# Second-layer low products in bf16, a dense plane for the weights' high part, and one ring of six raw-weight buffers

## The chip, the cores and the metric

The kernel runs on one core of a Trainium2 chip. The metric is the device time of one execution in microseconds (us); before the change it is 961.33 us, the median of three runs (959.22 to 962.11). The core's engines are named as the profile names them: PE (TensorE, matrix products), PEld (the weight loads of PE), DVE (VectorE), ACT (ScalarE), POOL (GpSimd) and SP (the engine that issues most DMAs).

## The reference

Attention with a hash mask, then a two-layer network with a squared ReLU, all in float32. Shapes: 4 batches, 8 heads, 768 rows, head size 64; the network has 3072 rows, width 512 and 2048 hidden columns.

```python
mask   = bucket(q) == bucket(k)                  # 6 hash bits of each row
scores = where(mask, 0.125 * q @ k.T, -1e9)
attn   = softmax(scores)
x      = (attn @ v) reshaped to 3072 x 512
h      = x @ w_in                                # first layer, 512 -> 2048
g      = s * relu(h)**2 + b
out    = g @ w_out                               # second layer, 2048 -> 512
```

## The kernel before, in words

Every value that enters a product is split into a high and a low part, so that a product of two float32 matrices becomes three products of narrower types: high by high, high by low, low by high. The weights come from memory as pairs of 32-bit words and are put together on the chip ("decoded").

The rows of one batch are cut into three chunks of 256. For each chunk the first layer (lines 788 to 790, f16, 256 moving columns) makes 256 hidden columns ("a pair" of 128) in one PSUM bank with 24 products. ACT then forms the square and writes the high part `gh` (lines 798 to 800, tile `ghb`), and POOL writes the low part `gl` (lines 801 and 802, tile `glb`). The second layer (line 815) adds the pair into two PSUM banks, one for each 128 rows: 12 products of 512 moving columns, where a slice of `gh` or `gl` is loaded as PE's weights and a row block of `w_out` moves through: 8 with `gh` (against the high and the low part of `w_out`), 4 with `gl` (against the high part). All 12 are in float32r ("fp32r"), which the profile's rows call f32. There are 96 pairs: 4 batches, 3 chunks, 8 pairs.

Attention (lines 485 to 743) runs beside it: scores (lines 615 and 616, fp32r, 384 columns), softmax on DVE, ACT and POOL, and the product with the values (lines 686 and 692, f16). Once the attention of all heads is done, only the two layers of the last chunks are left; this is the tail from about 798 us on.

All instructions are collected as steps with an estimated cost, a priority and the keys that they read and write. The class `Plan` simulates the engines with these costs, picks at each moment the ready step of the best priority, and the steps are issued in that order. A step with several ways (a copy on ACT, POOL or DVE) goes to the engine that would end it first. Costs therefore set the order: a second-layer product is entered as 0.2343 (line 817).

`decode(u, pr)` (line 358) loads and decodes one of 32 row blocks of weights, in four groups of eight: four of `w_in`, then four of `w_out`. The raw block of `w_in` lives in a ring of six buffers (`wr0` to `wr5`) until the whole group's scale is known and it is split into f16 (lines 427 to 432). The raw block of `w_out` lives in the buffer that its decoded form takes later (`w{u}`), so it needs no ring. Its decoded form is one tile of two float32r planes, high and low (lines 399 to 401). The load is issued by ACT's queue (line 377), and two loads at most are open at a time (`PACE`).

Of the kernel before, what the change touches and what calls it, by code (L numbers as in the profile page):

```python
# [11 lines left out]
F32R = mybir.dt.float32r  # L12
I32 = mybir.dt.int32
F16 = mybir.dt.float16
BF16 = mybir.dt.bfloat16
U32 = mybir.dt.uint32
AF = mybir.ActivationFunctionType
ALU = mybir.AluOpType
# [11 lines left out]
PE, DVE, ACT, POOL, SP = (mybir.EngineType.PE, mybir.EngineType.DVE, mybir.EngineType.Activation,  # L30
                          mybir.EngineType.Pool, mybir.EngineType.SP)
# [137 lines left out]
def lsh_attention_moe(ctx: ExitStack, tc, q, k, v, proj, w_in, w_out, s, b, out):  # L169
    nc = tc.nc  # L170
    B, H, S, D = q.shape
    DM, DF = w_in.shape
    P = 128
# [3 lines left out]
    CH = 256  # L177
    NCH = S // CH
    TPC = CH // P
    NC_ = DM // P  # L180
# [7 lines left out]
    wk = ctx.enter_context(tc.tile_pool(name="wk", bufs=1))  # L188
# [5 lines left out]
    plan = Plan()  # L194

    def f32(ap):
        return ap.bitcast(F32)

    def tile_(name, shape, dt=F32):
        return const.tile(shape, dt, name=name)  # L200

# [4 lines left out]
    def pe(cost, fn, r, w, pr):  # L206
        plan.add(PE, cost, fn, r, w, pr)
# [16 lines left out]
    def copy(n, out, src, r, w, pr, ways, slow=0.0):  # L224

        def fn(e):
            o, x = out(), src()
            (e.copy if e is nc.scalar else e.tensor_copy)(o, x)
        some(n, fn, r, w, pr, ways, slow)
# [52 lines left out]
    xsb = tile_("xsb", [P, 2, CH], F16)  # L282
    rb = tile_("rb", [P, 2 * CH])
    ghb = tile_("ghb", [P, 2, 2 * CH], F32R)
    glb = tile_("glb", [P, 2, 2 * CH], F32R)
    osb = tile_("osb", [P, 2, DM])
    pt = tb[:, 2].rearrange("p a h t q -> p (a h t q)")[:, 0:4 * DM].bitcast(F32).rearrange("p (t c) -> p t c", t=2)
    NST = 2
# [61 lines left out]
    dec, wt, held_raw = [], {}, []  # L350
# [7 lines left out]
    def decode(u, pr):  # L358
        src, key = dec[u]
        box = {}  # L360
        wi, kin = key[0] == "wi", u // (NC_ + 4) * NC_ + key[-1]
        tag = f"wr{kin % NWR}" if wi else f"w{u}"

        def new():
            box["t"] = wk.tile([P, 512, 2], I32, tag=tag, name=f"raw{u}")
# [1 line left out]
        def raw():  # L367
            return box["t"]

        def words(z):  # L370
            return box["t"].rearrange("p n t -> p (n t)")[:, z * 512:(z + 1) * 512]
        rk, wk_ = [("raw", tag)], [key + (0,), key + (1,)]
        g, gk = osb[:, u % 2, :], ("os", u % 2)
        gi = g.bitcast(I32)
        held = ["pjs"] if u == ND - 1 else []
        plan.add(None, 0.0, new, [], rk + held, pr - 5)
        plan.add(ACT, 0.1, lambda: nc.scalar.dma_start(raw(), src.rearrange("p (n t) -> p n t", t=2)), GATE(KK, AK) if u < PACE else [], rk + [("pace", u % PACE)], pr - 5, 524288 / RATE_DMA)
        plan.moves.add(len(plan.steps) - 1)
        if wi:
            n, j = key[1:]  # L380
# [13 lines left out]
        dve(512, lambda: nc.vector.scalar_tensor_tensor(sum_(), gi, 3, words(0), ALU.logical_shift_left, ALU.bitwise_or), [], rk + [gk], pr, 0.75)  # L394
        if not wi:
            def swap():
                wt[key] = wk.tile([P, 2, 512], F32R, tag=f"w{u}", name=f"w{u}")
            plan.add(None, 0.0, swap, [], rk + wk_, pr)
            copy(512, lambda: wt[key][:, 0], lambda: g, [gk], [key + (0,)], pr, (ACT, POOL))
            plan.any([(POOL, 1.4, lambda: nc.gpsimd.tensor_tensor(wt[key][:, 1], g, f32(wt[key][:, 0]), ALU.subtract)),  # L400
                      (DVE, 0.7, lambda: nc.vector.tensor_tensor(wt[key][:, 1], g, f32(wt[key][:, 0]), ALU.subtract))], [gk, key + (0,)], [key + (1,)], pr)
            return
        held_raw.append((words, rk, key))
        if j < NC_ - 1:
# [355 lines left out]
    def moe(bb, c, g0=0, g1=NF // 4):  # L760
        boxes = []
        fa, fz = 4 * g0, 4 * g1
        pr = 1e5 + 100.0 * nu[0]
# [12 lines left out]
        for f0 in range(fa, fz, 2):  # L776
            while nd[0] < f0 // 4 * 8 + 6 + f0 % 4:
                yield
            u = nu[0] % 2
            nu[0] += 1  # L780
            fill = 1e5 + 100.0 * nu[0]
            for j in range(2):
                hp, fs = bank[:, 5, j * CH:(j + 1) * CH], slice((f0 % 4 + j) * P, (f0 % 4 + j + 1) * P)
                for cc in range(NC_):
                    def mm(cc=cc, hp=hp, fs=fs, n=f0 // 4):
                        xc = boxes[cc][0]["t"][:, boxes[cc][1]]
                        w = wt[("wi", n, cc)]
                        nc.tensor.matmul(hp, w[:, 0, fs], xc[:, 0, :], start=(cc == 0), stop=False)  # L788
                        nc.tensor.matmul(hp, w[:, 1, fs], xc[:, 0, :], start=False, stop=False)  # L789
                        nc.tensor.matmul(hp, w[:, 0, fs], xc[:, 1, :], start=False, stop=(cc == NC_ - 1))  # L790
                    pe(0.327, mm, [boxes[cc][2], ("wi", f0 // 4, cc, 0), ("wi", f0 // 4, cc, 1)], [("b", 5)], fill)
            r, rk = rb, "r"
            gh, gl, hk, lk = ghb[:, u], glb[:, u], ("gh", u), ("gl", u)
            g4 = f0 // 4
            ds, dk = dsc[:, bb, g4:g4 + 1], ("ds", bb, g4)
            if c == 0 and f0 % 4 == 0:
                dve(1, lambda g4=g4, ds=ds: nc.vector.tensor_tensor(ds, vsc[:, bb, 1:2], wsc[:, g4, 1:2], ALU.mult), [("sc", bb), ("wsc", g4)], [dk], MP, 0.1)
            some(2 * CH, lambda e, r=r, ds=ds: e.activation(r, bank[:, 5, :], AF.Relu, scale=ds) if e is nc.scalar else e.tensor_scalar(r, bank[:, 5, :], ds, 0.0, ALU.mult, ALU.max), [("b", 5), dk], [rk], MP, (ACT, DVE))  # L798
            act(2 * CH, lambda r=r: nc.scalar.activation(r, r, AF.Square), [], [rk], MP)
            act(2 * CH, lambda r=r, gh=gh: nc.scalar.activation(gh, r, AF.Identity, bias=b_sb, scale=s_sb), [rk, "sb"], [hk], MP, 0.15)  # L800
            pool(2 * CH, lambda r=r: nc.gpsimd.tensor_scalar(r, r, s_sb, b_sb, ALU.mult, ALU.add), [hk, "sb"], [rk], MP, 0.77)  # L801
            pool(2 * CH, lambda r=r, gh=gh, gl=gl: nc.gpsimd.tensor_tensor(gl, r, f32(gh), ALU.subtract), [rk, hk], [lk], MP)  # L802

            end = bb == B - 1 and c == NCH - 1 and f0 == NF - 2
            for part in ((0, 1), (2,)) if HALVES and not end else ((0, 1, 2),):
                for jt in range(2 * TPC):
                    j, t = (jt % 2, jt // 2) if end else (jt // TPC, jt % TPC)
                    f = f0 + j

                    def mm2(f=f, j=j, t=t, gh=gh, gl=gl, part=part):  # L810
                        ts = slice(j * CH + t * P, j * CH + (t + 1) * P)
                        o = bank[:, 6 + t, :]
                        w = wt[("wo", f)]
                        for z in part:
                            nc.tensor.matmul(o, (gh, gh, gl)[z][:, ts], w[:, z % 2], start=(f == fa and z == 0), stop=(f == fz - 1 and z == 2))  # L815
                    ks_ = [[hk, ("wo", f, 0)], [("wo", f, 1)], [lk]]
                    pe(0.2343 * len(part), mm2, [k for z in part for k in ks_[z]] + [("wo", f, 0)], [("b", 6 + t)], fill + 150)
        for t in range(TPC):
            o, os_ = bank[:, 6 + t, :], osb[:, t]
            if fz < NF:  # L820
# [36 lines left out]
    for i in range(NSL):  # L857
        pr = 10.0 * i
        bb, h, c, w = slots[i]
# [31 lines left out]


FIRST = 0.5
CONV = (ACT, POOL)
CONVCOST = 0.95
RATE = 1.0
# [4 lines left out]
NWR = 6  # L901
# [46 lines left out]
```

## Time and profile before

| | us |
|---|---|
| median of three runs | 961.33 |
| lowest and highest | 959.22, 962.11 |
| the profiled execution | 960.13 |
| its span | 958.3 |
| PE busy | 921.6 (96%) |
| DVE, ACT, POOL busy | 606.2, 656.7, 614.2 |

The span is the time from the first to the last instruction of the program; 1.8 us of the profiled execution lie around it. A busy PE is not a PE at its peak: a product's record lasts until its results have drained, so records of products that follow each other overlap. How fast PE really goes is read from the distance between the starts of two products.

### The profile page before, as it was taken

How to read it: one execution, taken by the hardware profiler on the slowest of the kernel's cores; microseconds unless marked ns; L12 is line 12 of the kernel's file. 1: busy time of each engine (PE TensorE's matmuls, PEld its weight loads, DVE VectorE, ACT ScalarE, POOL GpSimd, SP SyncE). 2: the span in 40 equal slices, each digit the busy share in tenths (PEclk: the TensorE clock that was granted, in tenths of full speed). 3: DMA queues.
4: the chain of work that ended last, by engine and by line, in shares of the span. 5: the costliest groups of instructions: out<-in, count | busy, mean ns of one | idle time of the engine just before them, and what ended most of it. 6: DMA issues, size and time to landing. Idle time of an engine off the chain costs nothing.

```text
span 958.3 us, 18093 instructions
## 1 busy us (share of the span) xinstructions
PE 921.6 (96%) x6512; PEld 733.2 (77%) x6512; DVE 606.2 (63%) x1001; ACT 656.7 (69%) x1234; POOL 614.2 (64%) x706
## 2 busy tenths in 40 slices
PE   7999887999999999999999999999999999999997
PEld 5876666677667777877878778788778887888886
DVE  7688997888777777776767676768777752000000
ACT  3788886778786777677778777767777775444342
POOL 2467775686896756766777676767667775334332
PEclk8999999899999999999999999999999999999999
DMA  5378657647779898997898798888887875100000
GB/s 123 87 232 220 177 160 191 179 133 209 174 153 204 176 206 181 204 213 149 157 204 172 163 204 163 177 174 167 186 173 149 171 134 105 55 19 27 12 23 23
DMA packets 303721, 144.44 MB, mean 151 GB/s; under 512 B 264256, under 2 KB 286784, under 8 KB 303632
## 3 DMA queue, kind: packets, MB, share of 16 engines
q1 hardware_dynamic: 298432, 126.25, 60.5%
q10 hardware_dynamic: 5200, 17.05, 5.7%
q8 instruction: 51, 0.84, 0.3%
q14 instruction: 38, 0.31, 0.1%
HBM read 51.38 MB, written 14.16 MB: 68 GB/s over the span
## 4 chain that ended last, share of the span: by engine, by line
PE 70%; DVE 9%; POOL 7%; ACT 5%; issue 5%; DMA 2%; POOLq 0%; SPq 0%; ACTq 0%; DVEq 0%
PE bank L815 22%; PE bank L788 7%; PE bank L790 7%; PE bank L789 7%; PE bank L615 6%; PE bank L616 5%; PE bank L686 4%; PE bank L680 3%; PE bank L672 2%; PE bank L692 2%; POOL eb L640 2%; DVE st L620 2%; PE bank L485 2%; POOL glb L802 2%; ACT eb L621 1%
## 5 line engine op out<-in xcount | busy, mean ns | idle before, releaser
L640 POOL TENSOR_SCALAR eb<-eb,st 128x768 f32<-128x768 f32 x176 | 200.4, 1145 | 68.4 <-DVE st L631 51.8
L815 PE MATMUL bank<-w,ghb 128*128 128x512 f32 x768 | 213.6, 406 | 0.0
L788 PE MATMUL bank<-xc,wi 128*128 128x256 f16 x768 | 211.6, 276 | 0.3 <-ACT rb L798 0.3
L620 DVE TENSOR_REDUCE st<-bank 128x1 f32<-128x768 f32 x192 | 180.3, 952 | 49.6 <-PE bank L616 42.3
L790 PE MATMUL bank<-xc,wi 128*128 128x256 f16 x768 | 209.7, 273 | 0.0
L789 PE MATMUL bank<-xc,wi 128*128 128x256 f16 x768 | 209.7, 273 | 0.0
L621 ACT ACTIVATE eb<-bank,st 128x768 f32<-128x768 f32 x176 | 157.5, 896 | 65.2 <-DVE st L620 29.3
L801 POOL TENSOR_SCALAR rb<-rb,misc 128x512 f32<-128x512 f32 x96 | 84.8, 884 | 154.0 <-ACT ghb L800 146.4
L648 DVE SCALAR_TENSOR_TENSOR pb<-eb,pb 128x768 f16<-128x768 f32 x132 | 144.3, 1097 | 61.5 <-ACT pb L647 60.9
L798 ACT ACTIVATE rb<-bank,dsc 128x512 f32<-128x512 f32 x95 | 65.2, 687 | 149.1 <-PE bank L790 135.4
L615 PE MATMUL bank<-ks,aq 128*128 128x384 f32 x384 | 146.7, 382 | 10.8 <-ACT eb L621 5.2
L815 PEld LDWEIGHTS bank<-w,ghb 128*128 128x128 f32 x768 | 136.1, 189 | 21.2 <-issue 0.4
L802 POOL TENSOR_TENSOR glb<-rb,ghb 128x512 fp32r<-128x512 f32 x96 | 137.1, 1428 | 5.8
L616 PE MATMUL bank<-ks,bq 76*128 76x384 f32 x384 | 132.1, 344 | 0.8 <-DMA bq<-nat 0.8
L647 ACT ACTIVATE pb<-eb 128x768 f16<-128x768 f32 x132 | 110.1, 836 | 14.3 <-DMA tb<-pb 13.3
L815 PE MATMUL bank<-w,glb 128*128 128x512 f32 x384 | 113.0, 402 | 3.1 <-POOL glb L802 3.1
L788 PEld LDWEIGHTS <-wi 128*128 128x128 f16 x768 | 75.0, 98 | 44.5 <-issue 37.3
L615 PEld LDWEIGHTS bank<-ks,aq 128*128 128x128 f32 x384 | 74.5, 194 | 30.0 <-ACT eb L621 9.2
L838 DVE COPY osb<-bank 128x256 f32<-128x256 f32 x4 | 1.5, 420 | 133.7 <-PE bank L815 133.0
L815 PEld LDWEIGHTS bank<-w,glb 128*128 128x128 f32 x384 | 70.8, 189 | 19.5 <-POOL glb L802 4.9
L625 POOL TENSOR_SCALAR st<-st 128x2 f32<-128x2 f32 x96 | 41.8, 436 | 63.2 <-DVE st L620 58.4
L790 PEld LDWEIGHTS <-wi 128*128 128x128 f16 x768 | 75.2, 98 | 8.6
(137 smaller groups left out, 1510.2 us busy)
## 6 DMA issues: line engine op xcount, KB each, us to landing
ks<-aq SPq DMA_DIRECT2D x60, 192.0 KB
raw<-in_moe_w_in_dram ACTq DMA_DIRECT2D x16, 512.0 KB
raw<-in_moe_w_out_dram ACTq DMA_DIRECT2D x16, 512.0 KB
xc<-xd SPq DMA_DIRECT2D x60, 128.0 KB
nat<-in_q_dram SPq DMA_DIRECT2D x32, 192.0 KB
nat<-in_k_dram SPq DMA_DIRECT2D x32, 192.0 KB
vm<-in_v_dram SPq DMA_DIRECT2D x32, 192.0 KB
xd<-xsb SPq DMA_DIRECT2D x48, 128.0 KB
```

Source lines behind the costliest of these rows:

```text
L615: nc.tensor.matmul(o, aq[:, ts], ks[0][:, cols], start=True, stop=False)
L616: nc.tensor.matmul(o, bq[0:HR, ts], ks[1][0:HR, cols], start=False, stop=True)
L620: dve(S, lambda a=a, sc=sc: nc.vector.tensor_reduce(nm[:, a:a + 1], sc, AX.XY, ALU.max, negate=True), bk, [nk[a]], pr, 0.88)
L621: act(S, lambda a=a, sc=sc, e=e: nc.scalar.activation(e.rearrange("p (g n) -> p g n", g=2), sc, AF.Exp, bias=nm[:, a:a + 1], accum_out=z[: ...
L640: eng.tensor_scalar(e, e, rz[:, a:a + 1], u[:, a:a + 1], ALU.mult, ALU.add)
L647: act(S, lambda e=e, hi=hi: nc.scalar.mul(hi, e, TOP), [ek], [hk], pr)
L648: dve(S, lambda e=e, hi=hi, lo=lo: nc.vector.scalar_tensor_tensor(lo, e, TOP, hi, ALU.mult, ALU.subtract), [ek, hk], [("lo", n)], pr, 1.0)
L788: nc.tensor.matmul(hp, w[:, 0, fs], xc[:, 0, :], start=(cc == 0), stop=False)
L789: nc.tensor.matmul(hp, w[:, 1, fs], xc[:, 0, :], start=False, stop=False)
L790: nc.tensor.matmul(hp, w[:, 0, fs], xc[:, 1, :], start=False, stop=(cc == NC_ - 1))
L802: pool(2 * CH, lambda r=r, gh=gh, gl=gl: nc.gpsimd.tensor_tensor(gl, r, f32(gh), ALU.subtract), [rk, hk], [lk], MP)
L815: nc.tensor.matmul(o, (gh, gh, gl)[z][:, ts], w[:, z % 2], start=(f == fa and z == 0), stop=(f == fz - 1 and z == 2))
```

## The change

Line numbers behind the change are 4 to 6 higher than before (the second layer's line 815 becomes 821, the first layer's 788 to 790 become 794 to 796, the raw load's 377 becomes 381).

- `gl` is written as bf16. `w_out` is decoded into three tiles: the high part `w` in float32r, the low part `wl` in bf16, and `wp`, the high part once more in bf16, made by one copy more.
- High by high stays in float32r. High by low takes the upper 16 bits of each word of `gh`, read with a step of two (`top`), as bf16 weights against `wl`. Low by high is `gl` against `wp`, bf16 against bf16.
- The planner's cost of the two bf16 products is 0.2165 instead of 0.2343.
- All 32 raw blocks share the ring of six (`u % 6`). So a load waits until the block six places before it is done with.

```diff
+    def top(ap):
+        return ap.bitcast(BF16).rearrange("p (n t) -> p n t", t=2)[:, :, 1]
...
-    glb = tile_("glb", [P, 2, 2 * CH], F32R)
+    glb = tile_("glb", [P, 2, 2 * CH], BF16)
...
-        wi, kin = key[0] == "wi", u // (NC_ + 4) * NC_ + key[-1]
-        tag = f"wr{kin % NWR}" if wi else f"w{u}"
+        wi = key[0] == "wi"
+        tag = f"wr{u % NWR}"
...
-                wt[key] = wk.tile([P, 2, 512], F32R, tag=f"w{u}", name=f"w{u}")
-            plan.add(None, 0.0, swap, [], rk + wk_, pr)
-            copy(512, lambda: wt[key][:, 0], lambda: g, [gk], [key + (0,)], pr, (ACT, POOL))
+                wt[key] = [wk.tile([P, 512], dt, tag=f"{x}{u}", name=f"{x}{u}") for x, dt in (("w", F32R), ("wl", BF16), ("wp", BF16))[:2 + PLANE]]
+            plan.add(None, 0.0, swap, [], held + wk_, pr)
+            copy(512, lambda: wt[key][0], lambda: g, [gk], [key + (0,)], pr, (ACT, POOL))
...
+            if PLANE:
+                copy(512, lambda: wt[key][2], lambda: g, [gk], [key + (2,)], pr, (ACT, POOL, DVE))
...
-                            nc.tensor.matmul(o, (gh, gh, gl)[z][:, ts], w[:, z % 2], start=(f == fa and z == 0), stop=(f == fz - 1 and z == 2))
-                    ks_ = [[hk, ("wo", f, 0)], [("wo", f, 1)], [lk]]
-                    pe(0.2343 * len(part), mm2, [k for z in part for k in ks_[z]] + [("wo", f, 0)], [("b", 6 + t)], fill + 150)
+                            nc.tensor.matmul(o, (gh, top(gh), gl)[z][:, ts], (w[0], w[1], w[2] if PLANE else top(w[0]))[z], start=(f == fa and z == 0), stop=(f == fz - 1 and z == 2))
+                    ks_ = [[hk, ("wo", f, 0)], [("wo", f, 1)], [lk, ("wo", f, 2 if PLANE else 0)]]
+                    pe(sum((0.2343, 0.2165, 0.2165)[z] for z in part), mm2, [k for z in part for k in ks_[z]] + [("wo", f, 0)], [("b", 6 + t)], fill + 150)
```

On PE, in the tail, the second layer of one pair stands like this before (`w_2354` and `w_2398` are two row blocks of `w_out`, both planes in one tile):

```order
L790 MATMUL bank<-xc_2_1_0_9363,wi_3_235 128x256
L815 MATMUL bank<-w_2354,ghb 128x512 x4
L815 MATMUL bank<-w_2398,ghb 128x512 x4
L815 MATMUL bank<-w_2354,glb 128x512 x2
L815 MATMUL bank<-w_2398,glb 128x512 x2
L788 LDWEIGHTS wi_0_232
```

and its middle like this now, at the same place (`w_253` is a block's high plane, `wl_254` its low one, `wp_252` the dense bf16 plane of the pair's other block):

```order
L821 MATMUL bank<-w_253,ghb 128x512
L821 LDWEIGHTS ghb
L821 MATMUL bank<-wl_254,ghb 128x512
L821 MATMUL bank<-w_253,ghb 128x512
L821 LDWEIGHTS ghb
L821 MATMUL bank<-wl_254,ghb 128x512
L821 LDWEIGHTS glb
L821 MATMUL bank<-wp_252,glb 128x512
```

A float32r product carries its weight load in itself; a 16-bit product has one of its own ahead of it. Twelve float32r products in a row have become four that alternate with bf16 ones, and then four bf16 ones, of which the first is shown.

On ACT, in the decoding of the first group, the third load of a `w_out` block (`raw_209`) stood right behind the decoding of the first (`raw_207`):

```order
L386 ACTIVATE osb<-raw_207 128x512
L377 DMA raw_208<-in_moe_w_out_dram 128x1024
L386 ACTIVATE raw_207<-raw_207 128x512
L228 COPY xpb<-bank 64x128
L586 ACTIVATE vm,vmx<-vm 128x384
L228 COPY xpb<-bank 64x128
L621 ACTIVATE pb,st<-bank,st 128x768
L621 ACTIVATE eb,st<-bank,st 128x768
L228 COPY tb<-bank 128x512 x3
L377 DMA raw_209<-in_moe_w_out_dram 128x1024
```

Now the third and fourth (`raw_1293`, `raw_1308`) stand some thirty rows further on, behind the split of the group's `w_in` blocks (`wi_1_204` and `wi_2_205`):

```order
L433 ACTIVATE wi_1_204<-raw_200,wsc 128x512
L433 ACTIVATE wi_2_205<-raw_201,wsc 128x512
L627 ACTIVATE eb,st<-bank,st 128x768 x2
L232 COPY tb<-bank 128x512 x3
L381 DMA raw_1293<-in_moe_w_out_dram 128x1024
L381 DMA raw_1308<-in_moe_w_out_dram 128x1024
```

The two loads moved behind the split, because they take the buffers of the first two `w_in` blocks.

## Rows read from the trace of the kernel before

**Rows 1.** The page: span, and busy time of each engine

```profile
span 958.3 us, 18093 instructions
PE 921.6 (96%) x6512; PEld 733.2 (77%) x6512; DVE 606.2 (63%) x1001; ACT 656.7 (69%) x1234; POOL 614.2 (64%) x706
```

**Rows 2.** Stretches: length, PE, PEld, DVE, ACT, POOL busy; granted clock, DMA share, GB/s

```profile
0.00:300.00 300.00, 270.42 (x2042) 209.67 (x2043) 245.88 (x474) 225.00 (x479) 206.32 (x253) 0.97 0.66 172
300.00:798.00 498.00, 496.60 (x3443) 398.05 (x3440) 354.22 (x517) 364.58 (x656) 346.85 (x393) 1.00 0.85 175
798.00:958.00 160.00, 154.58 (x1031) 125.45 (x1030) 6.10 (x11) 67.10 (x99) 61.05 (x61) 1.00 0.13 35
```

**Rows 3.** The same for line 815 alone, first stretch: length, PE busy, PEld busy

```profile
0.00:300.00 300.00, 35.83 (x120) 20.98 (x120) 0.97 0.66 172
```

**Rows 4.** The page's groups of line 815: busy us, mean ns, idle before

```profile
L815 PE MATMUL bank<-w,ghb 128*128 128x512 f32 x768 | 213.6, 406 | 0.0
...
L815 PE MATMUL bank<-w,glb 128*128 128x512 f32 x384 | 113.0, 402 | 3.1 <-POOL glb L802 3.1
```

**Rows 5.** Timeline of PE, one pair of the tail: start, length, instruction

```profile
881.78 0.27 PE L790 MATMUL bank<-xc,wi 128*128 128x256 f16 x1
881.81 2.10 PE L815 MATMUL bank<-w,ghb 128*128 128x512 f32 x8
883.74 1.10 PE L815 MATMUL bank<-w,glb 128*128 128x512 f32 x4
884.69 0.29 PE L788 MATMUL bank<-xc,wi 128*128 128x256 f16 x1
884.81 0.27 PE L789 MATMUL bank<-xc,wi 128*128 128x256 f16 x1
```

**Rows 6.** Timeline of PE, fp32r products alone between f16 ones

```profile
691.79 0.60 PE L686 MATMUL bank<-tb,vb 128*128 128x256 f16 x4
692.15 0.48 PE L815 MATMUL bank<-w,glb 128*128 128x512 f32 x1
...
692.59 0.27 PE L789 MATMUL bank<-xc,wi 128*128 128x256 f16 x1
```

**Rows 7.** Timeline of PE, two fp32r products between f16 ones

```profile
907.28 0.27 PE L790 MATMUL bank<-xc,wi 128*128 128x256 f16 x1
907.31 0.71 PE L815 MATMUL bank<-w,ghb 128*128 128x512 f32 x2
...
907.98 0.27 PE L789 MATMUL bank<-xc,wi 128*128 128x256 f16 x1
```

**Rows 8.** Timeline of PEld, the weight load behind a run of fp32r products

```profile
884.21 0.19 PEld L815 LDWEIGHTS bank<-w,glb 128*128 128x128 f32 x1
884.68 0.10 PEld L788 LDWEIGHTS <-wi 128*128 128x128 f16 x1 [0.28 <-issue]
```

**Rows 9.** Timeline of PE, f16 products whose weight tile changes its width

```profile
261.82 0.60 PE L686 MATMUL bank<-tb,vb 128*128 128x256 f16 x4
262.35 0.52 PE L692 MATMUL bank<-tb,vb 128*64 128x256 f16 x6
```

**Rows 10.** Timeline of ACT and POOL, the making of gh and gl in the tail

```profile
883.53 0.82 ACT L800 ACTIVATE ghb<-rb,misc 128x512 fp32r<-128x512 f32 x1
885.30 1.27 POOL L802 TENSOR_TENSOR glb<-rb,ghb 128x512 fp32r<-128x512 f32 x1
```

**Rows 11.** Groups by form, copies and subtraction in the decoding of w_out

```profile
L401 DVE TENSOR_TENSOR w<-osb,w 128x512 fp32r<-128x512 f32 x7 | 6.6, 949 | 0.5 <-ACT w L228 0.3 <-POOL w L228 0.2
...
L228 POOL CAST w<-osb 128x512 fp32r<-128x512 f32 x8 | 6.0, 748 | 2.9 <-DVE osb L394 1.5 <-ACT aq L487 1.4
...
L228 ACT CAST w<-osb 128x512 fp32r<-128x512 f32 x8 | 5.0, 620 | 1.3 <-POOL w L400 1.1
```

**Rows 12.** Timeline of ACT: third w_out load, and the first group's split

```profile
76.63 0.33 ACTq L377 DMA_DIRECT2D raw<-in_moe_w_out_dram  x1
...
112.32 1.95 ACT L427 ACTIVATE wi<-raw,wsc 128x512 f16<-128x512 f32 x3 [0.41 <-DVE wsc L447]
```

More of the change, by code (lines that the diff above doesn't have):

```diff
@@ L371, in words @@
             return box["t"].rearrange("p n t -> p (n t)")[:, z * 512:(z + 1) * 512]
-        rk, wk_ = [("raw", tag)], [key + (0,), key + (1,)]
+        rk, wk_ = [("raw", tag)], [key + (z,) for z in range(3)]
         g, gk = osb[:, u % 2, :], ("os", u % 2)
@@ L375, in decode @@
         held = ["pjs"] if u == ND - 1 else []
-        plan.add(None, 0.0, new, [], rk + held, pr - 5)
+        plan.add(None, 0.0, new, [], rk, pr - 5)
         plan.add(ACT, 0.1, lambda: nc.scalar.dma_start(raw(), src.rearrange("p (n t) -> p n t", t=2)), GATE(KK, AK) if u < PACE else [], rk + [("pace", u % PACE)], pr - 5, 524288 / RATE_DMA)
@@ L396, in swap @@
             def swap():
-                wt[key] = wk.tile([P, 2, 512], F32R, tag=f"w{u}", name=f"w{u}")
-            plan.add(None, 0.0, swap, [], rk + wk_, pr)
-            copy(512, lambda: wt[key][:, 0], lambda: g, [gk], [key + (0,)], pr, (ACT, POOL))
-            plan.any([(POOL, 1.4, lambda: nc.gpsimd.tensor_tensor(wt[key][:, 1], g, f32(wt[key][:, 0]), ALU.subtract)),
-                      (DVE, 0.7, lambda: nc.vector.tensor_tensor(wt[key][:, 1], g, f32(wt[key][:, 0]), ALU.subtract))], [gk, key + (0,)], [key + (1,)], pr)
+                wt[key] = [wk.tile([P, 512], dt, tag=f"{x}{u}", name=f"{x}{u}") for x, dt in (("w", F32R), ("wl", BF16), ("wp", BF16))[:2 + PLANE]]
+            plan.add(None, 0.0, swap, [], held + wk_, pr)
+            copy(512, lambda: wt[key][0], lambda: g, [gk], [key + (0,)], pr, (ACT, POOL))
+            plan.any([(POOL, 1.4, lambda: nc.gpsimd.tensor_tensor(wt[key][1], g, f32(wt[key][0]), ALU.subtract)),
+                      (DVE, 0.7, lambda: nc.vector.tensor_tensor(wt[key][1], g, f32(wt[key][0]), ALU.subtract))], [gk, key + (0,)], [key + (1,)], pr)
+            if PLANE:
+                copy(512, lambda: wt[key][2], lambda: g, [gk], [key + (2,)], pr, (ACT, POOL, DVE))
             return
@@ L893 @@
 FIRST = 0.5
+PLANE = True
 CONV = (ACT, POOL)
```

## The prediction

> **What bounds the kernel now.** I read the page's head first, then the table of stretches, then the timeline of PE product by product, because records of products overlap and busy shares say little there.
>
> PE is busy for 96% of the span, no other engine for more than 69% [rows 1]. By stretches, PE is busy for 270 of the first 300 us, for 497 of the next 498, and to the end for 155 of 160, where DVE has nothing left to do and ACT and POOL are under half busy; the granted clock is 1.00 from 300 us on, the 2.4 GHz level [rows 2]. Of the 1152 products of the second layer (768 with `gh`, 384 with `gl`) [rows 4] only 120 lie in the first 300 us [rows 3]. So PE sets the pace wherever the changed products stand, and what a product saves or costs goes nearly one to one into the end.
>
> **What an fp32r product costs.** An f16 product of 256 columns follows the last one after 0.109 us (four of them start from 691.79, and the fp32r product behind them is recorded early, some 30 ns after the fourth, so I measure from f16 start to f16 start) [rows 6]. 256 columns at 2.4 GHz are 0.1067 us, so 2 ns are on top. A 16-bit product of 512 columns should then cost 0.216 us. This is an estimate: no 16-bit product of 512 columns runs before; twice 0.109 is its upper bound, 512 columns at that clock, 0.213, the lower. I take the same 0.216 as the floor of an fp32r product and ask what lies above it.
>
> - Twelve in a row: from 881.78 to 884.81 are 3.03 us [rows 5]. Taken off: two f16 products (0.218) and 12 x 0.2157 (2.588). 0.224 remain.
> - Two in a row: 907.28 to 907.98, 0.70 us [rows 7], less 0.218 and 0.431: 0.051 remain.
> - One alone: 691.79 to 692.59, 0.80 us [rows 6], less five f16 products (0.545) and 0.216: 0.039 remain.
>
> From two to twelve, ten products add 0.173, 17 ns each; and each run of them, however short, leaves about 20 ns more (0.016 by the run of two, 0.022 by the single one). The 20 ns lie where the run ends: the weight load of the next f16 product does not start while the last fp32r product streams; it starts at 884.68, after 0.28 us without any load, 4 ns before its own product [rows 8].
>
> So the change pays in two coins: 17 ns for each product that is no longer fp32r, and about 20 ns for each new place where a 16-bit product follows an fp32r one.
>
> **Part by part.**
>
> *The products.* 768 of 1152 become bf16: 768 x 17 ns = 13.1 us gained. But in each half of a pair's work every high-by-high product is now followed at once by a bf16 one. Counted in PE's order, 16-bit products follow fp32r ones at 234 places before and at 516 now: 384 are inside the second layer, and the others are attention's own. 282 x 20 ns = 5.6 us lost. Net 7.4 us gained. The tail's pair gives the same: 224 ns above the floor before, 4 x 37 = 148 now, 76 ns a pair, times 96 pairs 7.3 us. In other words, the alternating four and four gain nothing (37 ns against two times 17), and the gain comes from the `gl` products and from what they no longer bring with them. At the edges, 0.213 and 0.218 instead of 0.216 for 768 products move this by -2.3 and +1.5 us.
>
> *The bf16 weights of high by low.* They are read with a step of two elements; no row of before shows such a load. Bounds: as cheap as the dense f16 load behind a run (20 ns at the exit, above), or as dear as a load that is not hidden at all. The latter is seen where f16 products with 128 weight columns give way to ones with 64: the fourth L686 starts at 261.82 + 3 x 0.109 = 262.15, the next product at 262.35, 0.20 later instead of 0.109, 94 ns more [rows 9]. Cheaper than 20 would need a load ahead of time, the first rival. I take 20, because the dense load stands at the same kind of switch. The upper end costs 384 x 74 = 28.4 us more.
>
> The Trainium skill bears on this in "TensorE: Matmul & The Clock Gate", section "Weight-path perf modes — Fast Weight Load (FWL) and DoubleRow": loads of 128 weights that are not FP32 go fast, packed or strided, with a column step of up to 1,024 elements. By that rule the step of two costs nothing and the sum stays as it is; no run here shows it yet.
>
> *`gl` in bf16, from POOL.* POOL ends it at 885.30 + 1.27 = 886.57. PE wants it after the next 24 first-layer products and 8 products with `gh`, at 884.69 + 24 x 0.109 + 8 x 0.234 = 889.2 [rows 5, 10]. A shorter or longer write of the same elements is covered by 2.6 us; cost nothing. The pair gets shorter by only 0.08 us, so nothing becomes late there.
>
> *The dense planes.* 16 copies more: by the order 7 on ACT, 5 on DVE, 4 on POOL. By the rows that is 7 x 0.62 + 4 x 0.75 = 7.3 us on ACT and POOL, and at most 5 x 0.95 = 4.7 us on DVE (a DVE copy of this size isn't shown; the subtraction with two inputs bounds it) [rows 11]. All lie in the first 300 us, where these engines are busy for 246, 225 and 206 us [rows 2], so idle time could hide them all. Bounds 0 and 4.7, if DVE were the path throughout; nothing below 0, as they only add work. I take 1.0. In the subtraction and the copies only the type written changes; I price that at nothing, with the same cover.
>
> *The ring.* The third `w_out` load was issued at 76.6 us; now it needs the buffer of the first `w_in` block, which is free only after the group's split at 112.3 [rows 12]. So it is some 36 us later, and later groups wait in the same way, with whatever stands behind the load on ACT's queue placed by the planner accordingly. When attention has made 128 of its 384 L615 products, PE's order has 8 first-layer steps of three products and 12 second-layer products fewer in it than before: 8 x 3 x 0.109 + 12 x 0.234 = 5.4 us of work put off from a stretch where PE had gaps. At 160 it has 6 such steps and 12 products more than before: 4.8 us ahead. Bounds +5.4 and -4.8; I take 0.
>
> **Sum.** On the profiled execution: 960.1 - 7.4 + 1.0 = 953.7 us. It was 1.2 us below the median of 961.33; from the median it is 954.9. I say 954.5. With 15 to 22 ns at an exit and the edges above, this case reaches from 950 to 959.
>
> **The rivals.**
>
> *The exits are free.* If the next weight load ran beside the last fp32r product after all, only the first coin counts: 961.3 - 13.1 = 948.2 with no loss at the front. For it: a bf16 product streams for 0.216 us, twice as long as the f16 ones around the runs measured, so more can hide behind it. Against it: the 20 ns arise behind the fp32r product, which is as long as ever [rows 8]. The planner's two costs, 0.2343 and 0.2165, amount to the same case: 768 x 17.8 ns = 13.7 us.
>
> The same page of the Trainium skill, "TensorE: Matmul & The Clock Gate", section "Step-by-step: what each phase is for", has PE pull weight loads ahead of products in flight when they go to the background buffer. That would make the exits free. The trace disagrees at this switch: the load waits until the fp32r product has streamed [rows 8].
>
> *The strided load is slow (slower than before).* PE, at each of the 384 switches from high by high to high by low. If the load of every second 16-bit word takes longer, it can't hide, since it starts only after the fp32r product. The 7.4 us are used up by 7.4 / 0.384 = 19 ns, so it decides from 39 ns for an exit; at 55 ns the time is 968, at the 94 of the bound 954.9 + 28.4 = 983. For it: fp32r loads take 0.19 us and f16 loads 0.10 in the records [rows 8], so load time depends on what is read, and the strided read spans as many bytes as the fp32r one. Against it: 17 ns is all that an fp32r product pays, load included.
>
> *The front gives it back (no change).* The 5.4 us of deferred work are not made up, or exits cost some 30 ns (3.8 us more): 958.7 to 960.3. For it: DVE is busy for 82% of the first 300 us [rows 2]. Against it: the order is ahead again by 160.
>
> **Chances and range.** Less than 0.3%, 2.9 us, can't be told from no change here: 958.4 to 964.2. The forecast has 0.47, free exits 0.17, the slow load 0.20, the front or dear exits 0.16. Faster: the first two and a little of the last, 0.65. Slower: the slow load without its lowest part, 0.18. No change: 0.17. The range goes from 946, the free exits less the lower edge, to 965, where an exit costs about 46 ns; some 0.15 lie beyond.
>
> **What will tell.** In a pair of the tail: from the last f16 product to the second of the next pair 2.95 us instead of 3.03, with starts fp32r to bf16 to fp32r 0.47 apart by twos, and `gl` products 0.216 apart. 0.45 by twos would mean free exits; over 0.49 a slow load. All PE loads of bf16 `ghb` weights should read 0.10 us. PE should be full from 300 us on; if it gets there some 5 us later, the ring is the cause. I am wrong in the mechanism if the `gl` products stay at 0.23, or if PE has gaps of its own in the tail.

## The result, and the profile after

The changed kernel takes 971.54 us (median of six, 969.20 to 974.63), the kernel before 961.72 in the same series (six, 959.13 to 963.60). The ratio is 1.0105 with an interval of 1.0088 to 1.0123: about 10 us slower, where 7 us faster was forecast. The profiled execution has a span of 971.6 us; its head answers to [rows 1], its stretches to [rows 2].

The head of the page of the changed kernel:

```profile
span 971.6 us, 18091 instructions
PE 924.2 (95%) x6512; PEld 656.5 (68%) x6512; DVE 625.5 (64%) x1013; ACT 660.9 (68%) x1235; POOL 624.1 (64%) x714
```

The stretches of the changed kernel (columns as in [rows 2]; the last ends later with the span):

```profile
0.00:300.00 300.00, 265.73 (x1973) 197.63 (x1973) 240.71 (x470) 216.79 (x460) 208.15 (x253) 0.94 0.62 164
300.00:798.00 498.00, 490.67 (x3397) 346.92 (x3397) 364.58 (x515) 364.33 (x654) 342.92 (x388) 0.99 0.85 175
798.00:972.00 174.00, 167.81 (x1145) 111.92 (x1143) 20.18 (x30) 79.73 (x123) 73.00 (x74) 1.00 0.20 46
```

By 300 us PE has issued 69 products fewer than before (1973 against 2042), in the middle stretch 46 fewer, and the tail is 14 us longer: 114 more products are left for it. DVE and ACT did not get more to do in the first stretch, they did less (240.7 against 245.9 us, 216.8 against 225.0); POOL did 1.8 us more (208.2 against 206.3). So no engine is overloaded; the first stretch simply got less far.

The products themselves are as forecast. One pair of the tail, timeline of PE in the changed kernel (start, length, instruction), answering to [rows 5]:

```profile
896.59 0.27 PE L796 MATMUL bank<-xc,wi 128*128 128x256 f16 x1
896.62 0.47 PE L821 MATMUL bank<-w,ghb 128*128 128x512 f32 x1
896.94 0.39 PE L821 MATMUL bank<-wl,ghb 128*128 128x512 bf16 x1
896.98 0.58 PE L821 MATMUL bank<-w,ghb 128*128 128x512 f32 x1
897.40 0.39 PE L821 MATMUL bank<-wl,ghb 128*128 128x512 bf16 x1
...
898.57 1.03 PE L821 MATMUL bank<-wp,glb 128*128 128x512 bf16 x4
899.43 0.27 PE L794 MATMUL bank<-xc,wi 128*128 128x256 f16 x1
899.54 0.27 PE L795 MATMUL bank<-xc,wi 128*128 128x256 f16 x1
```

From the last f16 product to the second of the next pair are 899.54 - 896.59 = 2.95 us, the forecast number (3.03 before). By twos, bf16 start to bf16 start, are 897.40 - 896.94 = 0.46 to 0.47. The four `glb` products take 899.43 - 898.57 = 0.86, 0.215 each.

The page's groups of the second layer, answering to [rows 4], show the three kinds apart (busy us, mean ns, idle before):

```profile
L821 PE MATMUL bank<-w,ghb 128*128 128x512 f32 x384 | 177.4, 534 | 0.0
...
L821 PE MATMUL bank<-wl,ghb 128*128 128x512 bf16 x384 | 150.1, 391 | 0.0
...
L821 PE MATMUL bank<-wp,glb 128*128 128x512 bf16 x384 | 102.7, 380 | 4.3 <-POOL glb L808 4.3
```

`gl` from POOL makes PE wait for 4.3 us in all, 1.2 more than before: little of the loss lies there.

The weight loads of the same stretch, timeline of PEld:

```profile
896.93 0.10 PEld L821 LDWEIGHTS <-ghb 128*128 128x128 bf16 x1
...
897.40 0.10 PEld L821 LDWEIGHTS <-ghb 128*128 128x128 bf16 x1 [0.26 <-issue]
```

The strided load takes 0.10 us, like the dense one in [rows 8]. That agrees with the Trainium skill, "TensorE: Matmul & The Clock Gate", section "Weight-path perf modes — Fast Weight Load (FWL) and DoubleRow", by which loads of 128 weights that are not FP32 go fast, packed or strided. The strided load, too, starts only with its own product, after 0.26 us without any load. What the Trainium skill says on the same page in the section "Step-by-step: what each phase is for", that loads are pulled ahead of products in flight, does not show at this switch: at 401 of the 408 places where a bf16 load of line 821 follows a float32r one, it starts 4 or 5 ns before its own product.

To see work and idle time apart I added up PE's products over each trace: 16-bit ones at columns / 2.4 GHz + 2 ns, float32r ones at 17 ns more, and 20 ns at each switch from float32r to 16 bits; the rest of the span is idle time or time at half clock. Before: 875.3 + 83.0 us. After: 867.9 + 103.6. The 17 ns were measured on products of 512 columns and are an assumption for the narrower ones, but those are the same in both kernels and drop out of the differences: the work fell by the forecast 7.4 us; the rest grew by 20.6.

Where it grew shows in the time at which attention's L615 (now L621) products are reached:

| product number | before, us | after, us | later by |
|---|---|---|---|
| 64 | 106.6 | 105.8 | -0.8 |
| 96 | 163.6 | 172.0 | 8.4 |
| 160 | 316.1 | 332.1 | 15.9 |
| 192 | 385.8 | 402.5 | 16.8 |
| 384 | 786.0 | 809.4 | 23.4 |

Most is lost by 332 us, behind the decoding. A second loss follows at 420 to 432 us, timeline of PE in the changed kernel (in brackets the idle time before, and what ended it):

```profile
422.99 0.44 PE L621 MATMUL bank<-ks,aq 128*128 128x384 f32 x1 [0.39 <-DVE nat L512]
...
426.39 0.44 PE L621 MATMUL bank<-ks,aq 128*128 128x384 f32 x1 [1.08 <-ACT eb L627]
...
429.63 0.64 PE L622 MATMUL bank<-ks,bq 76*128 76x384 f32 x1 [1.13 <-DMA bq<-nat]
...
431.62 1.44 PE L692 MATMUL bank<-tb,vb 128*128 128x256 f16 x6 [0.72 <-DMA tb<-pb]
...
434.39 0.42 PE L794 MATMUL bank<-xc,wi 128*128 128x256 f16 x1
434.60 0.42 PE L795 MATMUL bank<-xc,wi 128*128 128x256 f16 x1
```

Up to 433 us there are no first-layer products between these. A batch has 192 first-layer steps; when the 192nd L615 product is issued, 21 were left before and only 10 after. My reading is that they are PE's filler, and that they run out here because attention is late; no run isolates this hole.

Part of the 20.6 us is the clock. Stretches of the changed kernel, columns as in [rows 2]:

```profile
420.00:429.70 9.70, 6.41 (x36) 4.02 (x34) 8.38 (x16) 6.19 (x12) 6.54 (x10) 1.00 0.98 223
429.70:436.50 6.80, 6.08 (x28) 4.03 (x29) 4.86 (x7) 3.56 (x8) 3.86 (x6) 0.50 1.00 217
```

PE is busy for only 6.41 of 9.70 us, then the granted clock is 0.50, the 1.2 GHz level, for 6.8 us, and the first-layer products in the timeline above start 0.21 us apart instead of 0.109. Over the whole span the granted clock is 0.989 before and 0.979 after, so some 21 and 41 us pass at 1.2 GHz. The products that start in these stretches come to 8.9 us before and 16.0 after by the prices above; at half the clock they take about as much again. By this estimate some 7 of the 20.6 us are half clock, and the others are idle time.

### The profile page after: what moved, and what is told of

Its sections match the earlier page's. It is cut to its first block, busy times and chain, and to the rows that moved or that the text cites. A ratio compares the mean times of both kernels' runs of the same rounds, so it can differ in the third digit from the quotient of the medians.

```text
span 971.6 us, 18091 instructions
## 1 busy us (share of the span) xinstructions
PE 924.2 (95%) x6512; PEld 656.5 (68%) x6512; DVE 625.5 (64%) x1013; ACT 660.9 (68%) x1235; POOL 624.1 (64%) x714
## 4 chain that ended last, share of the span: by engine, by line
PE 56%; POOL 14%; issue 11%; DVE 10%; ACT 6%; DMA 2%; POOLq 0%; SPq 0%; ACTq 0%; DVEq 0%
PE bank L821 15%; PE bank L621 5%; PE bank L794 5%; PE bank L796 5%; PE bank L795 5%; PE bank L622 5%; PE bank L692 4%; POOL glb L808 4%; POOL eb L646 3%; POOL rb L807 3%; DVE st L626 3%; PE bank L686 3%; PE bank L678 3%; PE bank L698 2%; ACT eb L627 2%
## 5 line engine op out<-in xcount | busy, mean ns | idle before, releaser
L646 POOL TENSOR_SCALAR eb<-eb,st 128x768 f32<-128x768 f32 x176 | 194.2, 1110 | 50.3 <-DVE st L637 44.8
L654 DVE SCALAR_TENSOR_TENSOR pb<-eb,pb 128x768 f16<-128x768 f32 x132 | 146.6, 1123 | 65.3 <-ACT pb L653 63.5
L821 PE MATMUL bank<-w,ghb 128*128 128x512 f32 x384 | 177.4, 534 | 0.0
L621 PE MATMUL bank<-ks,aq 128*128 128x384 f32 x384 | 156.5, 408 | 18.4 <-ACT eb L627 14.5
L821 PE MATMUL bank<-wl,ghb 128*128 128x512 bf16 x384 | 150.1, 391 | 0.0
L808 POOL TENSOR_TENSOR glb<-rb,ghb 128x512 bf16<-128x512 f32 x96 | 140.8, 1466 | 6.2
L821 PE MATMUL bank<-wp,glb 128*128 128x512 bf16 x384 | 102.7, 380 | 4.3 <-POOL glb L808 4.3
L621 PEld LDWEIGHTS bank<-ks,aq 128*128 128x128 f32 x384 | 75.7, 197 | 38.8 <-ACT eb L627 21.3
L821 PEld LDWEIGHTS <-ghb 128*128 128x128 bf16 x384 | 37.2, 97 | 86.6 <-issue 80.5
L631 POOL TENSOR_SCALAR st<-st 128x2 f32<-128x2 f32 x96 | 44.3, 462 | 66.5 <-DVE st L626 58.3
```

Source lines behind the costliest of these rows:

```text
L621: nc.tensor.matmul(o, aq[:, ts], ks[0][:, cols], start=True, stop=False)
L646: eng.tensor_scalar(e, e, rz[:, a:a + 1], u[:, a:a + 1], ALU.mult, ALU.add)
L654: dve(S, lambda e=e, hi=hi, lo=lo: nc.vector.scalar_tensor_tensor(lo, e, TOP, hi, ALU.mult, ALU.subtract), [ek, hk], [("lo", n)], pr, 1.0)
L821: nc.tensor.matmul(o, (gh, top(gh), gl)[z][:, ts], (w[0], w[1], w[2] if PLANE else top(w[0]))[z], start=(f == fa and z == 0), stop=(f == f ...
```

## The experiments

Three changes come together: other types in the products, 16 plane copies, one ring of six. The first runs take them apart. The recorded expectations name three theories. F: the shared ring delays the weights. P: the copies and the bf16 writing slow the first 300 us. C: the planner's lower costs draw a worse order.

**Planner's costs alone, ring alone.** The kernel before, with only the costs, or only the ring:

```diff
-                    pe(0.2343 * len(part), mm2, ...
+                    pe(sum((0.2343, 0.2165, 0.2165)[z] for z in part), mm2, ...
```

> The kernel before with the planner's costs of the changed one (0.2165 for two of three second-layer products, which still run in fp32r), nothing else. Theory C: slower than before by 5 to 17 us, with a hole of PE in the middle (the changed kernel has one of 8 us at 420 us). Theories F and P: 959 to 964.

Measured: 960.45 us, ratio 1.0001 (0.9990 to 1.0012). So theory C is out: a new cost, and the order redrawn by it, is free.

```diff
-        tag = f"wr{kin % NWR}" if wi else f"w{u}"
+        tag = f"wr{u % NWR}"
```

> The kernel before, with the ring of six for all raw blocks and nothing else of the change. Theory F (the shared ring delays the weights, PE runs short of products in the first 340 us and the loss, some 17 us, never comes back): 975 to 979 us, attention's 160th L615 product some 16 us later than before (316 us). Theory P (the extra copies and the bf16 writing slow the first 300 us) and theory C (the planner's lower costs draw another order that fits the engines worse): within 2 us of before, 960 to 964.

Measured: 975.62 us, ratio 1.0144 (1.0121 to 1.0168). That is what theory F forecast, though its reason is tested further down. The ring alone costs more than the whole change.

**Copies alone.** The kernel before with 16 copies of a decoded `w_out` block into a bf16 scratch that nobody reads:

```diff
+            copy(512, lambda: scr[:, u % 2], lambda: g, [gk], [("scr", u % 2)], pr, (ACT, POOL, DVE))
```

> The kernel before with 16 copies more, one for each w_out block, of the high part into a small bf16 scratch tile that nobody reads; ring, products and costs as before. Theory P (the copies slow the first 300 us, where DVE, ACT and POOL have little room): 964 to 970 us, with most of it there by attention's 96th L615 product. If the copies hide, as the prediction held: 959 to 963.

Measured: 977.45 us, ratio 1.0187 (1.0146 to 1.0228). So do the copies, of some 0.6 us each: more than either forecast.

**The changed products without ring, without planes, without both.** `RAWAT` puts the raw `w_out` blocks of the first two groups where later groups' f16 weights will stand, so that they wait for no buffer (the last two groups share some); without planes `gl` multiplies the upper halves of the float32r words, read with a step of two.

```diff
-        tag = f"wr{u % NWR}"
+        tag = f"wr{kin % NWR}" if wi else RAWAT[kin]
...
```

> The changed kernel without the ring's waits: raw blocks of w_out lie in the slots of the later groups' f16 weights, which are still empty, so that the first half of the loads stand where they stood before; products, planes and costs as changed. Theory F: PE's gain of 80 ns a pair (7.7 us) is left, 954 to 957 us, the 160th L615 within 4 us of before. Theories P and C: 968 to 973, as the changed kernel.

```diff
-PLANE = True
+PLANE = False
```

> The changed kernel without the dense plane: its ring stays, low by high reads the high part with a step of two. With freed_noplane (neither, 950.5), freed (copies alone, 966.5) and the changed kernel (both, 971.5) it closes a table of four. If ring and copies each cost 15 us by themselves, as they did on the kernel before, 964 to 968; if the ring costs only where the copies lengthen the decoding too, 950 to 957.

Both edits together:

> The kernel without the ring's waits (freed, 966.5 us), and without the dense plane: low by high reads the upper 16 bits of each word of the high part in place, as moving operand with a step of two. Theory P: the remaining loss goes, 953 to 957 us. If the copies are not the cause: 964 to 969. The starts of the gl products tell by themselves what a moving operand with a step of two costs: 0.216 us apart if it streams at full rate, 0.43 at half, and then far slower than before.

| changed products with | us | ratio to before |
|---|---|---|
| ring and planes (the change) | 971.54 | 1.0105 (1.0088 to 1.0123) |
| planes, no ring | 966.53 | 1.0069 (1.0048 to 1.0089) |
| ring, no planes | 972.41 | 1.0093 (1.0060 to 1.0127) |
| neither | 950.46 | 0.9892 (0.9866 to 0.9918) |

The four were measured in four series, so the ratios are the safer comparison. Planes without ring came out between the two forecasts, ring without planes above both, neither below both. Neither is the best version here, 10.5 us faster than before. Each of the two alone costs 17 (planes) or 19 us (ring) by the ratios, both together no more than the ring alone. So the two costs do not add, and the table does not tell how the loss of the changed kernel divides between them.

**Before's own buffers, strided reads on both sides.** `glb` in bf16, the planner's costs of the changed kernel, and both low products read the high 16 bits in place (strided_grouped, which the expectation names, stands further down):

```diff
-... (gh, gh, gl)[z][:, ts], w[:, z % 2], ...
+... (gh, top(gh), gl)[z][:, ts], (w[:, 0], top(w[:, 1]), top(w[:, 0]))[z], ...
```

> Strided_grouped (965.8 us) with the products alternating, as in the changed kernel: the kernel before, with both low products in bf16 read in place with a step of two, no copy, no ring. By PE's prices: 768 x 17 ns less 282 exits x 20 ns less 768 x 9 ns, 0.5 us faster than before, 958 to 962. If the groups of four make the order worse (PE in strided_grouped stood idle 12 us longer than before in spite of less work), it is below strided_grouped, although its PE work is larger by 5.8 us.

Measured: 958.82 us, ratio 0.9966 (0.9949 to 0.9984), as expected.

**When the plane is copied, and from what.** From the version with planes and no ring: the copy reads the float32r plane, so that the decoding buffer is free earlier; or the same copy is planned just ahead of the block's first use in the second layer.

```diff
-                copy(512, lambda: wt[key][2], lambda: g, [gk], [key + (2,)], pr, (ACT, POOL, DVE))
+                copy(512, lambda: wt[key][2], lambda: f32(wt[key][0]), [key + (0,)], [key + (2,)], pr, (ACT, POOL, DVE))
```

> Freed (966.5 us) with the copies in the same place and at the same priority, but read from the finished float32r plane, so that the decoding's buffer (two of them, in turn) is free earlier. If the copies cost because they hold that buffer and so the next block's decoding: 950 to 955. If they cost because they stand in the queues of engines that have no room there: 963 to 969.

Measured: 974.30 us, ratio 1.0122 (1.0098 to 1.0147): worse than both forecasts. Freeing the buffer earlier did not help; but the plan is drawn anew here too, so this run alone does not clear the buffer.

```diff
-            if PLANE:
-                copy(512, lambda: wt[key][2], lambda: g, ...
+            planes.add(key)
...
+                        copy(512, lambda key=key: wt[key][2], lambda key=key: f32(wt[key][0]), [key + (0,), boxes[-1][2]], [key + (2,)], fill, (ACT, POOL, DVE))
```

> Freed (966.5 us) with the same 16 copies at another time and from another source: each from the finished float32r plane instead of the decoding's buffer, which it so no longer holds, and only once the input of the first layer that needs it has come, at the lowest priority. Dense products at 0.216 us as in freed. If the copies cost by their time and place in the first 140 us: 946 to 952, below freed_noplane by the 9 ns that a moving operand with a step of two costs (384 x 9 ns = 3.5 us). If 16 copies cost some 14 us wherever they stand: 962 to 968.

Measured: 955.83 us, ratio 0.9931 (0.9909 to 0.9952). That is between the two forecasts. The same 16 copies at another place cost 11 to 19 us less.

**Order or engine time.** So far a copy's cost could be its time on an engine, and the ring's the waiting for buffers; or both could be the order of instructions, which the planner lays out once for all engines from its costs and keys. Four runs hold the order and change the rest, each against a partner. First, copies of 8 columns that the plan counts as 512: the order on every engine is that of the copies alone, nearly all of their engine time is gone.

```diff
+            copy(512, lambda: scr[:, u % 2, 0:8], lambda: g[:, 0:8], [gk], [("scr", u % 2)], pr, (ACT, POOL, DVE))
```

> The kernel before, laid out with 16 copies of 512 columns in the plan, but each copy moves 8 columns only; the order on every engine is that of the 16 dummy copies (977.5 us). If the order that the plan makes room with costs the 16.5 us, this stays at 973 to 978. If the copies' own engine time does, it falls to 960 to 963.

Measured: 979.20 us, ratio 1.0198 (1.0177 to 1.0218). Then full copies that the plan counts as nothing: the order is that of before, with the copies put in.

```diff
+            plan.any([(ACT, 0.0, lambda: keep(nc.scalar)), (POOL, 0.0, lambda: keep(nc.gpsimd)), (DVE, 0.0, lambda: keep(nc.vector))], [gk], [("scr", u % 2)], pr)
```

> The kernel before with the same 16 full copies, which the plan counts as taking no time; the order on every engine is that of before with the copies put in between. If the order costs, this is 961 to 966 (at most some 0.3 to 0.6 us a copy on DVE, POOL and ACT). If the copies' engine time costs, 975 to 978.

Measured: 962.86 us, ratio 1.0032 (1.0010 to 1.0055). Then the ring in the plan's keys only; each raw block keeps its own buffer:

```diff
-        rk, wk_ = [("raw", tag)], ...
+        rk, wk_ = [("raw", f"wr{u % NWR}")], ...
```

> The kernel before with each raw block in its own buffer as before, but planned as if the 32 shared six; the order on every engine is that of the ring alone (975.6 us). If the order costs, 972 to 978. If the waiting for buffers does, 960 to 964.

Measured: 976.72 us, ratio 1.0174 (1.0157 to 1.0191), no less than with buffers really shared. Last, the changed products, no ring, planes copied but counted as nothing:

```diff
-                copy(512, lambda: wt[key][2], lambda: g, [gk], [key + (2,)], pr, (ACT, POOL, DVE))
+                plan.any([(ACT, 0.0, lambda: dense(nc.scalar)), (POOL, 0.0, lambda: dense(nc.gpsimd)), (DVE, 0.0, lambda: dense(nc.vector))], [gk], [key + (2,)], pr)
```

> The changed products with their dense planes and the raw blocks not sharing six, the 16 plane copies counted as nothing in the plan; the order is that of the version without planes (950.5 us), with the copies put in between. If the order was what the copies cost (966.5 with them counted), this is 950 to 955, the dense planes giving back up to 3.5 us of the strided read. If their engine time was, 964 to 967.

Measured: 953.43 us, ratio 0.9939 (0.9924 to 0.9953); with the copies counted it was 966.53. All four fall where the order decides, the tiny copies 1.2 us above the range given.

The traces bear out that the orders were held. Within each of four pairs (copies alone and tiny copies; before and uncounted copies; ring alone and ring in the keys only; changed products with neither and with uncounted planes) the instructions of PE, DVE, ACT and POOL, named by operation and tiles, follow each other in the same order, the copies themselves aside (83 of PE's 6512 records are missing from the last trace). Between before and copies alone they do not. So the copies' own time is worth 3.1 us (1.0 to 5.3) on the kernel before, waiting for raw buffers nothing that shows, and the order costs the rest: 979.20 against 962.86, 976.72 against 959.76 for the kernel before, and 966.53 against 953.43. What is not held apart is which part of an order costs. With own buffers, too, the third `w_out` load stands at 105.9 us (76.6 before) and the last low part of a `w_out` block is finished at 317.3 (289.5 before), because the plan puts them there.

What a worse order looks like, with less work in it (both profiled executions are the quickest of their kernel, 958.27 and 975.86 us): stretches around the decoding, first with full copies in the order of before, then with tiny copies in the other order (length, PE, PEld, DVE, ACT, POOL busy, granted clock, DMA share, GB/s).

```profile
78.00:118.00 40.00, 33.71 (x290) 25.44 (x287) 34.93 (x70) 31.99 (x73) 32.56 (x42) 1.00 0.71 186
118.00:200.00 82.00, 70.73 (x576) 55.05 (x576) 72.69 (x139) 65.66 (x143) 58.56 (x72) 0.96 0.63 169
```

```profile
78.00:118.00 40.00, 31.72 (x263) 24.03 (x262) 29.91 (x62) 29.56 (x67) 27.77 (x34) 0.91 0.61 157
118.00:200.00 82.00, 70.53 (x546) 54.50 (x546) 61.73 (x122) 59.17 (x133) 51.75 (x65) 0.92 0.59 165
```

All engines do less in the same time, and the granted clock is lower. The 64th L615 product comes at 106.6 us in the first and 115.9 in the second, and the 384th at 785.3 and 802.6. The waits between 70 and 200 us say who waits for whom (us in total, times, longest), in the same sequence:

```profile
POOL st L629 <- DVE st L624: 13.1, 9, 3.3
...
DVE st L624 <- PE bank L620: 4.5, 6, 1.1
```

```profile
POOL st L627 <- DVE st L622: 16.8, 9, 5.4
DVE st L622 <- PE bank L618: 14.6, 11, 3.0
```

DVE waits 10 us more for the scores of PE. And PE waits for ACT. Timelines of the tiny copies, PE and then ACT:

```profile
97.61 0.69 PE L617 MATMUL bank<-ks,aq 128*128 128x384 f32 x1 [4.07 <-ACT pb L623]
```

```profile
96.18 0.33 ACTq L378 DMA_DIRECT2D raw<-in_moe_w_in_dram  x1
96.56 0.90 ACT L623 ACTIVATE pb<-bank,st 128x768 f32<-128x768 f32 x1 [2.11 <-DMA ks<-aq]
```

And those of the full copies in the good order:

```profile
93.67 0.45 PE L619 MATMUL bank<-ks,aq 128*128 128x384 f32 x1 [0.96 <-ACT pb L625]
```

```profile
92.63 0.90 ACT L625 ACTIVATE pb<-bank,st 128x768 f32<-128x768 f32 x1 [1.07 <-DVE st L624]
```

The exponential `pb` reads the score bank that PE wants next. In the poor order a raw load stands right ahead of it in ACT's queue, and its issue is held until 96.18, until a transfer `ks<-aq` is through; `pb` waits 2.11 us behind it and PE 4.07 behind `pb`, four times what it waits at the same place in the good order. The clock follows, in stretches of the tiny copies:

```profile
88.00:95.50 7.50, 5.03 (x31) 3.78 (x31) 7.27 (x12) 4.52 (x11) 5.15 (x7) 1.00 1.02 246
95.50:102.30 6.80, 4.69 (x22) 4.16 (x24) 3.31 (x7) 4.64 (x10) 4.78 (x7) 0.50 0.57 172
```

PE was busy for 5.03 of 7.50 us, then the granted clock is 0.50 for 6.8 us, where the good order has 1.00 throughout (78 to 118 us, above). By the same estimate as for the changed kernel, half clock costs 13.1 us in the tiny copies and 4.7 in the full ones: 8.4 of the 17.6 us between the two spans (974.1 and 956.5).

The held load is one such place among several; how the 9.3 us up to the 64th product fall to single instructions is not isolated.

**Fours instead of alternation.** The new switches cost 20 ns each; with all high by high first, then all high by low, a pair has one such switch instead of four. Tried on the change, on the version with planes and no ring, and on the strided one:

```diff
-            for part in ((0, 1), (2,)) if HALVES and not end else ((0, 1, 2),):
+            for part in ((0,), (1,), (2,)) if HALVES and not end else ((0, 1, 2),):
```

> The changed kernel with the second layer's products of a half pair in three groups of four (fp32r, then bf16 high by low, then bf16 low by high) instead of alternating. By the price of 20 ns for each fp32r product that a 16-bit one follows, three exits fewer a pair, 60 ns: the tail's pair 5.287 us instead of 5.347, in all 5.8 us less, 964 to 967 us, whatever the cause of the loss in the first 340 us. If the exit's price were a property of the strided load and not of the switch, nothing would change.

> Freed (966.5 us) with the second layer's products in groups of four. By the exits 5.8 us less, 960.7. The changed kernel with the same edit gained only 1.5 us, with a new hole of PE at 826 to 837 us behind a transposing DMA; if such holes come with any new order, 962 to 968.

> The kernel before with its tiles and its ring; only the two low products change: both operands' upper 16 bits are read in place with a step of two (gl is written as bf16), in groups of four, and the costs are the changed kernel's. No copy, no ring, no other load. A pair then has one run of four fp32r products: 88 ns above the floor instead of 224, 136 ns a pair, 13 us: 946 to 950 us if a moving operand with a step of two streams at full rate and if the loss of the changed kernel came from ring and copies alone. If the loss came from cheaper products as such (attention isn't paced by PE, and PE runs out of second-layer work): 955 to 961.

Measured: 970.02 us (ratio 1.0101, 1.0083 to 1.0120), 966.85 (1.0066, 1.0044 to 1.0088) and 965.77 (1.0056, 1.0038 to 1.0074), against 971.54, 966.53 and 958.82 without. Only the second falls in a range given, that of new holes; the first and the third are slower than any forecast. The pair itself got its gain, in the timeline of PE of the first of them:

```profile
897.94 0.27 PE L796 MATMUL bank<-xc,wi 128*128 128x256 f16 x1
897.97 1.18 PE L821 MATMUL bank<-w,ghb 128*128 128x512 f32 x4
898.99 1.04 PE L821 MATMUL bank<-wl,ghb 128*128 128x512 bf16 x4
899.86 1.03 PE L821 MATMUL bank<-wp,glb 128*128 128x512 bf16 x4
900.72 0.27 PE L794 MATMUL bank<-xc,wi 128*128 128x256 f16 x1
900.83 0.27 PE L795 MATMUL bank<-xc,wi 128*128 128x256 f16 x1
```

900.83 - 897.94 = 2.89 us, 60 ns below 2.95, so 5.8 us for 96 pairs. The time does not show it; in the strided version it rises by 7 (9 by the ratios). New gaps stand in its place, for example in the same kernel:

```profile
826.83 0.39 PE L821 MATMUL bank<-wp,glb 128*128 128x512 bf16 x1 [0.72 <-POOL glb L808]
...
831.42 0.52 PE L698 MATMUL bank<-tb,vb 128*64 128x256 f16 x6 [2.46 <-DMA tb<-pb]
```

Why the planner places the steps so was not tried.

## Why the prediction was wrong

*The products* were right: 7.4 us less work on PE, 2.95 us for a pair, no dearer strided load, 1.2 us more waiting for `gl`. The version with neither ring nor planes is 10.5 us below before (7.6 between the profiled spans), but that is no proof of the price: its `gl` products read with a step of two, which costs 3.5 us of the gain (last section), so by PE's prices it should gain some 4. No run accounts for the other 6 us or so; a luckier order would explain them.

*The dense planes*: "I take 1.0", bounds 0 and 4.7. For the copies' engine time this about holds (3.1 us, with 1.0 to 5.3, on the kernel before). But a copy also enters the plan. This step failed: counted there it draws another order, and that costs some 16 us by itself: 979.2 with tiny copies in that order, 962.9 with full ones in the old order.

*The ring*: "Bounds +5.4 and -4.8; I take 0". This step failed most. I counted how many PE steps stand ahead of an attention product in the new order and priced the difference as work put off. That says how much work stands before it, not when the operands come: the order of the ring alone brings the 160th product 15.4 us later and the end 17 us later (976.72 against 959.76) with own buffers throughout. The late `w_out` load that I bounded was real, but waiting for its buffer was not what cost; whether the lateness that the plan gives it does is open.

On the kernel before each step alone costs more than the forecast gain; in the changed kernel, where both act and their costs do not add, no run divides the loss between them.

Both steps rest on one assumption that I did not write down: that an order drawn anew is as good as the old one, so that only work added and waits for buffers count. Changing the planner's costs alone shows that this can hold (1.0001); the ring and the copies, which touch the front where DVE, ACT, POOL and PE hand attention's rows round in turn, show that it need not. The sum also left the time at 1.2 GHz as it was; it rose from some 21 to 41 us.

*The rival "the front gives it back"* named the right place, with 0.16, and what stood against it, "the order is ahead again by 160", rests on the same count of steps, right as a count and no measure of time: the 160th product comes 15.9 us later. It was also sized too small: it ended at no change, with 3.8 to 5.4 us, where idle time and half clock grew by 20.6. The slower case that I did price, the slow strided load, has no part in it. What I gave as a sign, PE full some 5 us later, pointed the right way, at a third of the size.

## What to carry to other kernels

Where one planner lays out the order of all engines, 16 copies of 0.6 us can cost 16 us by the order alone; price it with the order held fixed (count the new work as nothing, or keep the old keys), and then ask for the order separately. Busy shares that fall on every engine at once were the sign of a poor order here: nothing is overloaded, the queues wait for each other; a granted clock that falls with them adds to the bill. The version to keep here has bf16 low products, no dense planes and no shared ring: 950.46 us, some of which its order may have given it.

## What the runs showed of the hardware

A moving bf16 operand that is read with a step of two is a little slower than a dense one. Timeline of PE, the four `gl` products without planes:

```profile
877.21 1.06 PE L826 MATMUL bank<-w,glb 128*128 128x512 bf16 x4
```

1.06 us instead of 1.03 in three steps from start to start are 10 ns a product; over all of them the starts are 0.224 to 0.225 apart against 0.215 to 0.216. So the planes save 384 x 9 ns = 3.5 us on PE, less than their 16 copies cost even when the order is kept: 953.43 with them, 950.46 without (ratios to before 0.9939, with 0.9924 to 0.9953, and 0.9892, with 0.9866 to 0.9918). The same step of two in a weight load costs nothing that shows.
